# A fused top-k attention and feed-forward kernel: another order for the first pair's loads, transposes and scores

## The chip, the cores and the metric

The kernel runs on one core of one Trainium2 chip. The metric is the device time of one execution in microseconds (us); the number for the kernel before is the median of three runs. A profile comes with it: one execution recorded by the hardware profiler, in which times count from the start of the span. TensorE is called PE in it, VectorE DVE, ScalarE ACT, GpSimd POOL, and SyncE, which issues the transfers, SP.

## What is computed

Eight batches of eight heads, 576 positions and a head size of 64 go through an attention that keeps only the 32 largest scores of each row. The 4,608 rows that come out, 512 wide, go through a feed-forward with a gate.

```python
scores = scale * np.matmul(q, k.transpose(0, 1, 3, 2))
kth = np.partition(scores, -top_k, axis=-1)[..., -top_k:-top_k + 1]
scores = np.where(scores >= kth, scores, -1000000000.0)
attn = np.exp(scores - np.max(scores, axis=-1, keepdims=True))
attn = attn / (np.sum(attn, axis=-1, keepdims=True) + 1e-09)
x = np.matmul(attn, v)            # then (B, H, S, D) -> (B*S, H*D)
h = x @ w_in
out = (h * np.clip(h + 3.0, 0.0, 6.0) / 6.0) @ w_out
```

Queries, keys and values are float32. The two weights reach the kernel in eight bytes an element and are turned into float32 on the chip.

## The kernel before

**Pairs.** Two heads of a batch are a `Pair`. `load` (lines 146 to 158) brings its keys and queries into one tile, `landed`, with six transfers, all issued by SyncE: two heads of k, k's left rows, two heads of q, q's left rows. The 576 positions are 512 and 64 left over; the left rows of k and q share the ninth 128x128 tile of `landed`. `transpose` (lines 171 to 183) turns the nine tiles on TensorE into one PSUM tile, `big`, of five banks, of which there is one. ScalarE then copies the columns out: 1,024 of them for the keys and queries (line 179), 64 of the queries' left part (line 180), and the keys' left part into `kr` (line 183, twice).

**Duos.** Two pairs of a batch and 128 query rows are a `Duo`. `scores` (lines 201 to 244) multiplies queries by the left keys (line 232) and by the 512 keys of each head (line 238) into `big`, and ScalarE copies the result into `sc` (line 239 for the 512 columns of each head, line 242 for the left ones). A row of `sc` that belongs to one head and one query is 576 wide.

**Top k.** `top` is VectorE's work: MAX8 finds the eight largest of a row (line 256), MATCH_REPLACE8 takes them out (line 260), four rounds for 32 values. Then GpSimd computes `shift`, ScalarE does `exp` and the sum `den`, VectorE its `inverse` (line 293), GpSimd the `weights` (lines 303 and 312), SyncE a transposing transfer (`flip`), ScalarE or GpSimd `join` (line 324), and TensorE `values` (line 344).

**Weights.** `convert` (lines 96 to 125) turns one chunk of 512 columns into float32 in four steps, and there are 32 chunks: sixteen of `w_in`, then sixteen of `w_out`. Step one issues the load of the words into a tile `st`. Step two computes `a` and `y` on ScalarE (lines 108 and 111) and clamps `a` on GpSimd (line 109). Step three shifts and merges bits on VectorE (lines 117 and 118). Step four adds the two on GpSimd (line 123). `a` and `y` come from the pool `g`, which has eight buffers and also holds the gates `g` of the feed-forward (line 378). `convert_step` moves several chunks on by one step: it adds the chunk that VectorE had in the step before, does step three for the next one, step two for a later one, and issues one more load with `land`.

**Order.** The order of the work is the program's own: every engine takes its instructions as they are written. After a start that is written out (lines 521 to 533), the main loop goes over the duos, and for each over eight rounds of `top`, four for each of the duo's two pairs. One such round, `8 * m + i`, is called a slot here. Each slot has a round of `top`, one `convert_step`, and parts of earlier duos at fixed distances (`early`, `usual`, `behind`, `soon`). `piece` puts pieces of the feed-forward into the slots as they become due. Three times before the loop `convert_step` is called, so in slot `s` the chunk `s + 1` is on VectorE, `s + 3` on ScalarE, and `s` is added.

Of the kernel before, what the change touches and what calls it, by code (L numbers as in the profile page):

```python
# [10 lines left out]
F32 = mybir.dt.float32  # L11
# [18 lines left out]
def kernel(  # L30
# [9 lines left out]
    nc = tc.nc  # L40
    P = nc.NUM_PARTITIONS
    B, H, S, D = q.shape
    DM, FF = moe_w_in.shape
    J = S // P
    JP = J * P
    R = S - JP
# [6 lines left out]
    def pool(name, bufs, **kw):  # L53
        return ctx.enter_context(tc.tile_pool(name=name, bufs=bufs, **kw))
# [12 lines left out]
    ps_w = pool("ps_w", 3, space=PSUM)  # L67
    ctx.enter_context(tc.manual_schedule())

    def const(shape, name):  # L70
        return consts.tile(shape, F32, tag=name, name=name)

    ident = const([P, P], "ident")
# [4 lines left out]
    w_out = const([P, NFC, DM], "w_out")  # L78
# [9 lines left out]
    def big():  # L88

        return ps_big.tile([P, 5 * 512], F32, tag="big", name="big")  # L90
# [48 lines left out]
    class Pair:  # L139
# [3 lines left out]
            self.b, self.hp = b, hp  # L143
            self.vm, self.vr, self.kr = vms[hp], vrs[hp], krs[b % 2 * NHP + hp]

        def load(self):
            h0 = 2 * self.hp
            t = self.landed = kqpool.tile([P, 2 * J + 1, 2, D], F32, tag="kq", name="landed")
            for i, src in enumerate((k, q)):
                for hh in range(2):  # L150
                    nc.sync.dma_start(
                        t[:, i * J : (i + 1) * J, hh, :],
                        src[self.b, h0 + hh, 0:JP, :].rearrange("(p j) d -> p j d", j=J),
                    )
                nc.sync.dma_start(
                    t[i * R : (i + 1) * R, 2 * J, :, :],
                    src[self.b, h0 : h0 + 2, JP:S, :].rearrange("h s d -> s h d"),
                )
# [9 lines left out]
                    self.vr[hh * R : (hh + 1) * R, hh, :], v[self.b, h0 + hh, JP:S, :]  # L168
                )

        def transpose(self):
            kq = kqpool.tile([P, JP + S], F32, tag="kq", name="kq")
            self.kT, self.qT = kq[:, 0:JP], kq[:, JP : JP + S]
            ps = big()
            for j in range(2 * J + 1):
                rows = self.landed[:, j, :, :].rearrange("p h d -> p (h d)")
                nc.tensor.transpose(ps[:, j * P : (j + 1) * P], rows, ident[:])
            c0 = 2 * JP
            nc.scalar.copy(kq[:, 0:c0], ps[:, 0:c0])
            nc.scalar.copy(kq[:, c0 : c0 + R], ps[:, c0 + R : c0 + 2 * R])  # L180
            for hh in range(2):
                d = slice(hh * D, (hh + 1) * D)
                nc.scalar.copy(self.kr[d, hh, :], ps[d, c0 : c0 + R])

    class Duo:

# [14 lines left out]
        def scores(self, us=(0, 1)):  # L201

            if us[0] == 0:
                self.sc = scpool.tile([P, 2, 2 * (S + R)], F32, tag="sc", name="sc")
                self.den = mpool.tile([P, 2, 2], F32, tag="den", name="den")
            sc, nu = self.sc[:, us[0] : us[-1] + 1, :], len(us)
            ps = big()
            heads = [slice(0, D), slice(D, P)]
            qs = slice(self.qt * P, min(self.qt * P + P, S))
            banks = ps[:, 0 : 4 * 512].rearrange("p (n s) -> p n s", s=512)  # L210
            left = ps[:, 4 * 512 :]
            if self.rest:


                quarters = [
                    (i, hh, d, heads[u ^ hh])
                    for i, u in enumerate(us)
                    for hh, d in enumerate(heads)
                ]
                for i, hh, d, to in quarters:  # L220
                    pr = self.pairs[us[i]]
                    nc.tensor.matmul(banks[to, i, :], pr.qT[d, qs], pr.kT[d, :])
                for i, hh, d, to in quarters:
                    pr = self.pairs[us[i]]
                    nc.tensor.matmul(banks[to, 2 + i, 0:R], pr.qT[d, qs], pr.kr[d, hh, :])
                nc.gpsimd.memset(sc[:, :, S : S + R], 0.0)
                nc.scalar.copy(sc[:, :, 0:JP], banks[:, 0:nu, :])
                nc.scalar.copy(sc[:, :, JP:S], banks[:, 2 : 2 + nu, 0:R])
                return
            for i, u in enumerate(us):  # L230
                pr = self.pairs[u]
                nc.tensor.matmul(
                    left[:, i * P : (i + 1) * P], pr.qT[:, qs], pr.kr[:].rearrange("p h r -> p (h r)")
                )
            for i, u in enumerate(us):
                pr = self.pairs[u]
                for hh, d in enumerate(heads):
                    nc.tensor.matmul(banks[:, 2 * i + hh, :], pr.qT[d, qs], pr.kT[d, :])  # L238
            nc.scalar.copy(  # L239
                sc.rearrange("p u (h s) -> p (u h) s", h=2)[:, :, 0:JP], banks[:, 0 : 2 * nu, :]  # L240
            )
            nc.scalar.copy(  # L242
                sc[:, :, JP : JP + P], left[:, 0 : nu * P].rearrange("p (u r) -> p u r", r=P)
            )

        def row(self, u, t):
            return self.sc[:, u, t * S : (t + 1) * S]
# [162 lines left out]
    duos = []  # L410
# [17 lines left out]
    left = 0  # L428
# [63 lines left out]
    def land(count=1):  # L492

        for _ in range(min(count, len(chunks))):
            c = convert(*chunks.pop(0))
            next(c)
            landing.append(c)

    def convert_step():


        for c in adding:
            next(c, None)
        adding.clear()
        if len(converting) >= 2 or not landing:
            for c in converting[:1]:
                next(c)
            adding.extend(converting[:1])
            del converting[:1]
        if landing:  # L510
            c = landing.pop(0)
            next(c)
            converting.append(c)
        land()

    def pair_at(m, first):

        b, at = divmod(m, per_batch)
        return pairs[b + 1][at - first] if b + 1 < B and 0 <= at - first < NHP else None

    first = pairs[0]
    first[0].load()
    land(2)
    first[1].load()
    first[0].transpose()
    convert_step()
    duos[0].scores((0,))
    convert_step()
    first[2].load()
    convert_step()  # L530
    first[1].transpose()
    duos[0].scores((1,))
    land()

# [28 lines left out]
    def parts(slot, late=None):  # L563

        for m, part in sorted(queued.get(slot, []), key=lambda x: x[1][:-1] != "shift"):
            if late is not None and (part[:-1] in ("inverse", "weights")) != late:
                continue
            if part == "values":
                values(m)
            elif part == "place":  # L570
                place(m)
            else:
                getattr(duos[m], part[:-1])(int(part[-1]))

    due = 0.0
    for m in range(ND + 3):
        u = duos[m] if m < ND else None
        for i in range(8):
            if u:
                u.top(i // 4, i % 4)  # L580
            if m < 4:
                parts(8 * m + i, False)
            convert_step()
            if m == 0 and i == 0:
                first[3].load()
            if m == 0 and i in (1, 2):
                first[i + 1].transpose()
            if i == (4 if m == 0 else 1) and m + 1 < ND:
                duos[m + 1].scores()
            if m < 4:  # L590
                parts(8 * m + i, True)
            else:
                parts(8 * m + i)
            if m == 0 and i in (1, 4):
                for p in duos[i // 4].pairs:
                    p.load_values()
            if i == 0:
                p = pair_at(m, 4)
                if p:
                    p.load()  # L600
            if i == 3 and u and u.pairs[0].b and 1 <= m % per_batch <= 2:
                for p in duos[m - 1].pairs:
                    p.load_values()
            if i == 5:
                p = pair_at(m, 5)
                if p:
                    p.transpose()

            due += ((left > 0) + (left >= 24) / 8 + (left >= 48) / 8) / (2 if u and u.rest else 1)
            piece(int(due))  # L610
            due -= int(due)
# [36 lines left out]
```

## Time and profile before

| | |
|---|---|
| time, median of three runs | 1577.45 us (1576.88 to 1578.07) |
| span of the profiled execution | 1576.1 us |
| busy: TensorE matmul | 1442.0 us (91%) |
| busy: VectorE | 1466.6 us (93%) |
| busy: ScalarE | 1097.2 us (70%) |
| busy: GpSimd | 1142.7 us (73%) |
| mean of a MAX8 on a row of 576 | 747 ns |
| first MAX8 | 13.73 us |

A row of the timeline gives the start, the length, the engine, the line, what is written from what, the shape, the count, and in brackets how long the engine had been idle and what ended that. A line of the waits gives who waited for whom, the total in us, the number of times, and the longest. A wait for several things is put down to what came last. Busy shares are means over stages with different limits, so the start and the weight conversion are read from their own stretches.

### The profile page before, as it was taken

The page shows a single profiled execution, that of the slowest core. Times are in us where ns is not written, and L with a number is a line of the kernel's source. Part 1 is how long each engine was busy: PE and PEld are TensorE (multiplying, and loading weights), DVE is VectorE, ACT ScalarE, POOL GpSimd, SP SyncE. Part 2 cuts the span into 40 slices and gives each one's busy share as a digit, 9 for nine tenths or more (in the row PEclk, how much of TensorE's full clock was granted, in tenths as well). Part 3 has the DMA queues.
Part 4 walks back from the last instruction along what each step waited for, and adds up shares of the span by engine and source line. Part 5 has one row for each costly group of instructions (what it writes and reads, how often), then busy time and mean ns, then how long its engine had stood idle before and what let it go on. Part 6 is the DMA issues. An engine that isn't in the chain of part 4 may idle for free.

```text
span 1576.1 us, 28787 instructions
## 1 busy us (share of the span) xinstructions
PE 1442.0 (91%) x10272; PEld 1031.7 (65%) x10272; DVE 1466.6 (93%) x3105; ACT 1097.2 (70%) x1865; POOL 1142.7 (73%) x1264
## 2 busy tenths in 40 slices
PE   5355799879999999998999999998999999999899
PEld 3142666567767777676777777776777777776675
DVE  6999999999999999999999999999999999999700
ACT  6675776777877777777776786777776786777521
POOL 4868687777867777867687777867687777867831
PEclk9577899989999999999999999999999999999999
DMA  8552544444444543545254544445254443533410
GB/s 237 158 183 42 116 83 83 89 94 98 73 96 86 101 84 78 99 87 117 54 104 81 98 88 83 94 91 113 58 105 81 98 88 82 103 58 68 83 22 14
DMA packets 450319, 144.49 MB, mean 92 GB/s; under 512 B 433280, under 2 KB 441472, under 8 KB 450176
## 3 DMA queue, kind: packets, MB, share of 16 engines
q1 hardware_dynamic: 450176, 142.65, 43.7%
q8 instruction: 81, 1.33, 0.3%
q14 instruction: 62, 0.51, 0.1%
HBM read 45.09 MB, written 9.44 MB: 35 GB/s over the span
## 4 chain that ended last, share of the span: by engine, by line
DVE 74%; PE 12%; POOL 6%; issue 4%; ACT 2%; SPq 1%; DMA 1%; POOLq 0%
DVE m L256 39%; DVE wk L260 34%; PE acc L391 5%; PE h L371 5%; POOL e L312 1%; PE pv L344 1%; POOL a L109 1%; POOL sc L303 1%; ACT sc L284 1%; POOL w_in L123 1%; DVE den L293 1%; PE big L238 1%; POOL w_out L123 1%; DMA st<-in_moe_w_in_dram 1%; POOL eT L324 1%
## 5 line engine op out<-in xcount | busy, mean ns | idle before, releaser
L256 DVE MAX8 m<-wk 128x8 f32<-128x576 f32 x864 | 613.6, 747 | 2.2
L391 PE MATMUL acc<-w_out,g 128*128 128x512 f32 x1152 | 518.2, 601 | 18.1 <-POOL g L386 18.1
L371 PE MATMUL h<-xT,w_in 128*128 128x128 f32 x4096 | 482.9, 278 | 18.3 <-ACT xT L354 18.3
L371 PEld LDWEIGHTS h<-xT,w_in 128*128 128x128 f32 x4096 | 472.5, 194 | 40.6 <-issue 18.4
L260 DVE MATCH_REPLACE8 wk<-m,wk 128x576 f32<-128x576 f32 x576 | 424.0, 743 | 0.0
L303 POOL TENSOR_SCALAR sc<-sc,den 128x576 f32<-128x576 f32 x288 | 213.2, 750 | 241.2 <-DVE den L293 223.4
L391 PEld LDWEIGHTS acc<-w_out,g 128*128 128x128 f32 x1152 | 213.5, 191 | 265.5 <-issue 238.6
L312 POOL COPY e<-sc 128x2304 uint16<-128x2304 uint16 (+1 forms) x192 | 320.0, 1676 | 10.1
L279 ACT ACTIVATE sc<-sc,m 128x576 f32<-128x576 f32 x288 | 209.8, 774 | 76.3 <-DVE m L256 75.9
L284 ACT ACTIVATE sc<-sc,shift 128x576 f32<-128x576 f32 x288 | 220.2, 767 | 52.1 <-POOL shift L272 50.0
L324 ACT COPY eT<-t 128x2304 uint16<-128x2304 uint16 (+1 forms) x82 | 216.0, 2634 | 44.5 <-DMA t<-e 39.8
L344 PE MATMUL pv<-eT,vm 128*64 128x128 f32 (+1 forms) x2560 | 164.1, 273 | 58.7 <-ACT eT L324 44.0
L260 DVE MATCH_REPLACE8 wk<-m,sc 128x576 f32<-128x576 f32 x288 | 212.0, 743 | 0.0
L344 PEld LDWEIGHTS pv<-eT,vm 128*64 128x64 f32 x2560 | 135.1, 141 | 110.3 <-ACT eT L324 48.2
L324 POOL COPY eT<-t 128x2304 uint16<-128x2304 uint16 (+1 forms) x78 | 203.6, 2610 | 4.5 <-DMA t<-e 4.3
L256 DVE MAX8 m<-sc 128x8 f32<-128x576 f32 x288 | 203.4, 744 | 1.5 <-ACT sc L242 1.5
L386 POOL TENSOR_TENSOR g<-g,hs 128x512 f32<-128x512 f32 x144 | 184.8, 1283 | 12.1
L379 ACT ACTIVATE g<-h,three 128x512 f32<-128x512 f32 x144 | 98.3, 683 | 133.8 <-PE h L371 123.1
L238 PE MATMUL big<-kq 64*128 64x512 f32 x512 | 136.1, 651 | 0.0
L239 ACT COPY sc<-big 128x2048 f32<-128x2048 f32 (+1 forms) x65 | 119.2, 1833 | 17.4 <-PE big L238 17.2
L385 POOL TENSOR_SCALAR g<-g 128x512 f32<-128x512 f32 x144 | 89.0, 618 | 51.9 <-ACT g L379 40.7
L401 ACT ACTIVATE o<-acc 128x512 f32<-128x512 f32 x36 | 21.4, 594 | 89.1 <-PE acc L391 89.1
(47 smaller groups left out, 1087.3 us busy)
## 6 DMA issues: line engine op xcount, KB each, us to landing
landed<-in_k_dram SPq DMA_DIRECT2D x64, 128.0 KB, 2.9
landed<-in_q_dram SPq DMA_DIRECT2D x64, 128.0 KB, 2.9
st<-in_moe_w_in_dram SPq DMA_DIRECT2D x16, 512.0 KB, 5.0
vm<-in_v_dram SPq DMA_DIRECT2D x64, 128.0 KB, 2.3
st<-in_moe_w_out_dram SPq DMA_DIRECT2D x16, 512.0 KB, 6.2
out_dram<-o SPq DMA_DIRECT2D x32, 256.0 KB, 2.4
t<-e SPq DMA_TRANSPOSE x160, 4.6
landed<-in_k_dram SPq DMA_DIRECT2D x32, 32.0 KB, 2.5
```

The source lines that it names most:

```text
L238: nc.tensor.matmul(banks[:, 2 * i + hh, :], pr.qT[d, qs], pr.kT[d, :])
L256: nc.vector.max(self.m[u][:, t, 8 * r : 8 * r + 8], self.cur[t])
L260: nc.vector.match_replace(wk, self.m[u][:, t, 8 * r : 8 * r + 8], self.cur[t], LOWEST)
L279: nc.scalar.activation(row, row, AF.Prelu, bias=m[:, t, TOP_K - 1 : TOP_K], scale=-1.0, alpha=FLAT)
L284: nc.scalar.activation(row, row, AF.Exp, bias=self.less[u][:, t : t + 1], scale=-scale / FLAT, accum_out=self.den[:, u, t : t + 1],)
L303: nc.gpsimd.tensor_scalar(row, row, self.den[:, u, t : t + 1], 1.0, ALU.mult, ALU.mult)
L312: nc.gpsimd.tensor_copy(halves[:, :, to : to + c1 - c0], words)
L324: copy(eT[:, 0 : self.nb, :] .rearrange("p c q -> p (c q)") .bitcast(U16) .rearrange("p (x h) -> p h x", h=2), self.t16[u][:, 0 : 2 * self ...
L344: nc.tensor.matmul(pv[hh * D : (hh + 1) * D, u * w : (u + 1) * w], pr.vm[:, hh, c, :] if c < J else pr.vr[:, hh, :], rhs, start=(c == 0), ...
L371: nc.tensor.matmul(h[:, (f - f0) * P : (f - f0 + 1) * P], w_in[:, i, f * P : (f + 1) * P], xT[:, i, :], start=(i == 0), stop=(i == NHP - 1),)
L386: nc.gpsimd.tensor_tensor(g[:], g[:], hs[:], ALU.mult)
L391: nc.tensor.matmul(acc[:], gs[f // nf][:, f % nf * P : (f % nf + 1) * P], w_out[:, f, :], start=(f == 0), stop=(f == NFC - 1),)
```

## The change

It touches the start of the kernel, before the main loop is in its steady order. It is meant to let VectorE begin its top-k earlier, with TensorE out of its slow clock by the first scores and the first batch's keys and queries at hand. It does six things.

- The first pair's queries are issued by ScalarE's queue while SyncE issues its keys.
- A warm-up is put first: VectorE clears a part of `w_out`, and TensorE multiplies it with itself twice. The result is not used.
- The first pair is transposed into three tiles of the pool `ps_w` in place of `big`: keys, then the first queries together with the left tile, then the other queries. Only what the first scores need is copied at once; the other two copies (`later`) come after the scores.
- For the first half of the first duo the left scores are copied first and each head's 512 columns by themselves, so that VectorE can begin with one head.
- The loads of all four pairs of the first batch stand ahead of most weight chunks: pair 1 and pair 2 before the second chunk, pair 3 before the loop and not in slot 0.
- `convert_step` is called twice before the loop and not three times.

```diff
--- before.py
+++ after.py
@@ -143,16 +143,17 @@
             self.b, self.hp = b, hp
             self.vm, self.vr, self.kr = vms[hp], vrs[hp], krs[b % 2 * NHP + hp]
 
-        def load(self):
+        def load(self, queue=None):
+
             h0 = 2 * self.hp
             t = self.landed = kqpool.tile([P, 2 * J + 1, 2, D], F32, tag="kq", name="landed")
-            for i, src in enumerate((k, q)):
+            for i, (src, eng) in enumerate(((k, nc.sync), (q, queue or nc.sync))):
                 for hh in range(2):
-                    nc.sync.dma_start(
+                    eng.dma_start(
                         t[:, i * J : (i + 1) * J, hh, :],
                         src[self.b, h0 + hh, 0:JP, :].rearrange("(p j) d -> p j d", j=J),
                     )
-                nc.sync.dma_start(
+                eng.dma_start(
                     t[i * R : (i + 1) * R, 2 * J, :, :],
                     src[self.b, h0 : h0 + 2, JP:S, :].rearrange("h s d -> s h d"),
                 )
@@ -168,19 +169,41 @@
                     self.vr[hh * R : (hh + 1) * R, hh, :], v[self.b, h0 + hh, JP:S, :]
                 )
 
-        def transpose(self):
+        def transpose(self, first=False):
+
             kq = kqpool.tile([P, JP + S], F32, tag="kq", name="kq")
             self.kT, self.qT = kq[:, 0:JP], kq[:, JP : JP + S]
+            c0 = 2 * JP
+
+            def turn(ps, tiles):
+                for i, j in enumerate(tiles):
+                    rows = self.landed[:, j, :, :].rearrange("p h d -> p (h d)")
+                    nc.tensor.transpose(ps[:, i * P : (i + 1) * P], rows, ident[:])
+
+            def copy_left(ps):
+                for hh in range(2):
+                    d = slice(hh * D, (hh + 1) * D)
+                    nc.scalar.copy(self.kr[d, hh, :], ps[d, 0:R])
+
+            if first:
+
+                ps = [ps_w.tile([P, 512], F32, tag="w", name="kqp") for _ in range(3)]
+                turn(ps[0], range(J))
+                turn(ps[1], [J, 2 * J])
+                turn(ps[2], range(J + 1, 2 * J))
+                nc.scalar.copy(self.kT, ps[0][:])
+                nc.scalar.copy(kq[:, JP : JP + P], ps[1][:, 0:P])
+                copy_left(ps[1][:, P:])
+                self.later = [
+                    (kq[:, JP + P : c0], ps[2][:, 0 : JP - P]),
+                    (kq[:, c0 : c0 + R], ps[1][:, P + R : 2 * P]),
+                ]
+                return
             ps = big()
-            for j in range(2 * J + 1):
-                rows = self.landed[:, j, :, :].rearrange("p h d -> p (h d)")
-                nc.tensor.transpose(ps[:, j * P : (j + 1) * P], rows, ident[:])
-            c0 = 2 * JP
+            turn(ps, range(2 * J + 1))
             nc.scalar.copy(kq[:, 0:c0], ps[:, 0:c0])
             nc.scalar.copy(kq[:, c0 : c0 + R], ps[:, c0 + R : c0 + 2 * R])
-            for hh in range(2):
-                d = slice(hh * D, (hh + 1) * D)
-                nc.scalar.copy(self.kr[d, hh, :], ps[d, c0 : c0 + R])
+            copy_left(ps[:, c0:])
 
     class Duo:
 
@@ -236,12 +259,15 @@
                 pr = self.pairs[u]
                 for hh, d in enumerate(heads):
                     nc.tensor.matmul(banks[:, 2 * i + hh, :], pr.qT[d, qs], pr.kT[d, :])
-            nc.scalar.copy(
-                sc.rearrange("p u (h s) -> p (u h) s", h=2)[:, :, 0:JP], banks[:, 0 : 2 * nu, :]
-            )
-            nc.scalar.copy(
-                sc[:, :, JP : JP + P], left[:, 0 : nu * P].rearrange("p (u r) -> p u r", r=P)
-            )
+            copies = [
+                (sc.rearrange("p u (h s) -> p (u h) s", h=2)[:, :, 0:JP], banks[:, 0 : 2 * nu, :]),
+                (sc[:, :, JP : JP + P], left[:, 0 : nu * P].rearrange("p (u r) -> p u r", r=P)),
+            ]
+            if us == (0,):
+                (to, src), rest = copies
+                copies = [rest, (to[:, 0, :], src[:, 0, :]), (to[:, 1, :], src[:, 1, :])]
+            for copy in copies:
+                nc.scalar.copy(*copy)
 
         def row(self, u, t):
             return self.sc[:, u, t * S : (t + 1) * S]
@@ -519,16 +545,25 @@
         return pairs[b + 1][at - first] if b + 1 < B and 0 <= at - first < NHP else None
 
     first = pairs[0]
-    first[0].load()
-    land(2)
+
+
+    nc.vector.memset(w_out[:, 0, :], 0.0)
+    ps = big()
+    for _ in range(2):
+        nc.tensor.matmul(ps[:, 0:DM], w_out[:, 0, 0:P], w_out[:, 0, :])
+    first[0].load(nc.scalar)
     first[1].load()
-    first[0].transpose()
+    land()
+    first[2].load()
+    land()
+    first[0].transpose(first=True)
+    duos[0].scores((0,))
+    for copy in first[0].later:
+        nc.scalar.copy(*copy)
     convert_step()
-    duos[0].scores((0,))
+    first[3].load()
+    first[1].transpose()
     convert_step()
-    first[2].load()
-    convert_step()
-    first[1].transpose()
     duos[0].scores((1,))
     land()
 
@@ -581,8 +616,6 @@
             if m < 4:
                 parts(8 * m + i, False)
             convert_step()
-            if m == 0 and i == 0:
-                first[3].load()
             if m == 0 and i in (1, 2):
                 first[i + 1].transpose()
             if i == (4 if m == 0 else 1) and m + 1 < ND:
```

## The prediction

> **What bounds the kernel now.** I read the page's chain of waits first, then VectorE's waits, then the timeline of the first 14 us and of the stretch around 137 us.
>
> The chain by engine, from the page:
>
> ```profile
> DVE 74%; PE 12%; POOL 6%; issue 4%; ACT 2%; SPq 1%; DMA 1%; POOLq 0%
> ```
>
> VectorE (DVE) holds three quarters of the chain; the end is TensorE working off its queue after VectorE's last top-k. VectorE's waits over the whole span (total us, times, longest):
>
> ```profile
> DVE a L117 <- POOL a L109: 13.6, 2, 10.3
> DVE den L293 <- ACT den L289: 7.0, 2, 6.7
> DVE m L256 <- ACT sc L242: 1.5, 1, 1.5
> ```
>
> The 10.3 is before the first MAX8, 0.3 of the 7.0 is at 32.8 us, the 6.7 is in the tail, and 3.3 is at 137 us. Otherwise VectorE never idles, so a microsecond won before its first MAX8 is a microsecond of the total, unless a later wait takes it back. The start, in the timeline (start, length, what):
>
> ```profile
> 4.13 0.63 SPq L155 DMA_DIRECT2D landed<-in_q_dram  x1
> 4.45 1.09 PE L177 MATMUL big<-ident,landed 128*128 128x128 f32 x4 [4.45 <-DMA landed<-in_k_dram]
> 6.81 1.30 PE L177 MATMUL big<-ident,landed 128*128 128x128 f32 x5 [1.28 <-DMA landed<-in_q_dram]
> 8.15 1.01 ACT L179 COPY kq<-big 128x1024 f32<-128x1024 f32 x1 [6.15 <-PE big L177]
> 9.16 0.43 ACT L183 COPY kr<-big 64x64 f32<-64x64 f32 x2
> 9.69 0.77 PE L232 MATMUL big<-kr,kq 128*128 128x128 f32 x2 [1.58 <-ACT kr L183]
> 10.39 2.08 PE L238 MATMUL big<-kq 64*128 64x512 f32 x4
> 12.52 1.01 ACT L239 COPY sc<-big 128x1024 f32<-128x1024 f32 x1 [1.52 <-PE big L238]
> 13.43 0.27 ACT L242 COPY sc<-big 128x128 f32<-128x128 f32 x1
> 13.73 1.42 DVE L256 MAX8 m<-sc 128x8 f32<-128x576 f32 x2 [1.53 <-ACT sc L242]
> ```
>
> It is one serial chain: q's landing, transposes, copies, scores, copies, MAX8. Around 137 us, where the last weight chunks are converted:
>
> ```profile
> 134.52 0.69 ACT L379 ACTIVATE g<-h,three 128x512 f32<-128x512 f32 x1 [9.12 <-POOL w_out L123]
> 135.57 0.67 ACT L108 ACTIVATE a<-st 128x512 f32<-128x512 f32 x1
> 136.40 0.61 POOL L109 TENSOR_SCALAR a<-a 128x512 f32<-128x512 f32 x1 [1.91 <-ACT a L108]
> 137.05 1.49 DVE L117 TENSOR_SCALAR a<-a 128x512 uint32<-128x512 uint32 x1 [3.30 <-POOL a L109]
> 139.87 1.99 PE L238 MATMUL big<-kq 64*128 64x512 f32 x8
> 142.83 1.41 DVE L256 MAX8 m<-wk 128x8 f32<-128x576 f32 x2
> 144.01 2.52 POOL L123 TENSOR_TENSOR w_out<-a,y 128x512 int32<-128x512 int32 x2
> 144.16 1.40 DVE L256 MAX8 m<-sc 128x8 f32<-128x576 f32 x2
> ```
>
> Here the gates g and the conversion's a and y compete for the eight g buffers: three chunks in flight (six) and two g fill them, so ScalarE sits 9.12 us until an add (L123) frees one, the next chunk's clamp is late, and VectorE waits 3.30. This stretch matters below.
>
> **What the Trainium skill says.** "TensorE: Matmul & The Clock Gate", Part 1: TensorE starts at half clock and is released after a busy window of about 3.4 us that is free-running; that is what the warm-up is for. The trace agrees: four L238 take 2.08 us at 10.39, eight take 1.99 at 139.87. Part 4 there says that transposes hardly count as busy for that gate; no row here shows it. "DMA: Bandwidth & Descriptors", section "Issuing engines are not separate DMA queues": a second issuing engine saves only issue time, the same 16 engines carry the data. "SBUF — State Buffer", section "Who interferes with whom": some VectorE forms and GpSimd lock each other out for a whole instruction; here L117 takes 0.41 at its shortest and 1.49 beside a GpSimd add.
>
> **The change, part by part.**
>
> *q on ScalarE's queue.* Issues cost about 0.64 us each on SyncE; six end at 4.76 and TensorE has q at 6.81, 2.05 later. Two queues of three end at 2.77, so 4.8. By bandwidth: 157 GB/s at a share of 0.69 (window 3 to 4 us) is 228 GB/s at full share, 576 KB take 2.5 us from about 2.2, so 4.7. I take 5.0. If ScalarE issues only after its table load (1.28 us from 0.72) it is 6.1; the load's row carries the line of the first copy, so I expect it behind the issues.
>
> *Warm-up.* A 128x512 memset on VectorE is bounded by its rows of that shape, 0.41 and 0.68; done at 1.5. Two float32 matmuls of 512 columns are four passes; a pass of L238 is about 0.85 cold (two heads' passes run side by side, so its four take 2.08): to 4.95. Both are beside the loads. k's four transposes follow, 1.09, to 6.05; q's first and the left tile about 0.45 more, to 6.5. ScalarE copies k (512 columns; 1.01 for 1024 and 0.27 for 128 give 0.59) 6.05 to 6.65, then q's 128 columns and two kr, 0.48 (0.43 before with 64), to 7.15. The other four transposes' columns are copied later, off the path.
>
> *Scores and split copies.* L183's end to L238's start is 0.80 cold, about 0.4 warm; L238 2.08 cold, half of 1.99 plus 0.1 = 1.1 warm. The left copy now hides under L238, and MAX8 needs just one head's 512 columns: 0.05 + 0.59 + 0.03, against 1.01 + 0.27 in sequence. First MAX8: 7.15 + 0.4 + 1.1 + 0.67 = 9.3 warm, 10.7 cold. The window's phase and the transposes decide; I take 9.8. **Gain 13.73 - 9.8 = 3.9.**
>
> *Loads ahead, slots 0 to 4* (a slot is one pass of the inner loop). SyncE issues: k of pair 0 to 2.8, pair 1 to 6.7, chunk 0 to 7.3, pair 2 to 11.3, chunks 1 and 2 to 12.4, pair 3 to 16.4, chunk 3 to 17.0. It lands 2.05 + about 0.8 later, 19.8; at the 5.0 us median of the page from its issue, 21.4. Behind that wait on ScalarE stand pair 2's copies (1.45), nine transposes on TensorE (2.18), pair 3's copies (1.45) and exp (29.58 to 32.77, 3.2): 19.8 + 1.15 + 1.45 + 2.18 + 1.45 + 3.2 = 29.2. VectorE reaches its first reciprocal at 9.8 + (32.5 - 13.73) = 28.6, less about 0.6 for conversions that meet fewer GpSimd adds: 28.0. It waits 1.2, against 0.3. **Cost 0.9 - 0.6 = 0.3.**
>
> *One conversion step fewer ahead of the loop.* Two instead of three, so each chunk is converted one slot later. Before, chunk 0's L117 and L118 lay in VectorE's idle time (11.18); now all 32 pairs lie in the dense stretch, the last in slot 31, where there was none. 0.41 + 0.68 = 1.09 at least. Slots 23 to 30 keep their relations, so the 3.30 wait stays. But the last chunk's a now comes in slot 29, with six buffers held by two chunks and two g: it waits for slot 29's add, the first of the pair at 144.01, done 145.3. ScalarE to 146.0, GpSimd's clamp to 146.65. VectorE is there at 144.16: **wait 2.5, plus 1.09, plus contention with the next add (0 to 1.1; I take 0.5): 4.1.** Behind the waiting L117 stand all later MAX8. ScalarE's join at 141.94 slips too, but values come seven slots later.
>
> *Dropped load in slot 0, `later` copies:* beside VectorE's work, nothing.
>
> **Sum:** 1577.45 - 3.9 + 0.3 + 4.1 = 1578.0.
>
> **The rivals.**
> - *Start gain kept.* The last chunk finds its buffer in time and costs 1.1 to 1.7. For it: buffers may be handed out otherwise than I think. Against: the count above, and the same shortage at 134.52. 1577.45 - 3.9 + 0.3 + 1.4 = 1575.2; with a warm TensorE and no longer reciprocal wait 1574.0.
> - *The old wait goes too.* A chunk's shift loosens the knot at 137: another 3.3 less, 1571.9. Against: the same buffers are held in the same slots.
> - *Loads become the bound, slower.* Cold TensorE (gain 3.0), chunk 3 landing at 21.4 or later (reciprocal wait 1.5 more), full contention in slot 31 (4.7): 1577.45 - 3.0 + 1.8 + 4.7 = 1581.0. For it: from 10 to 30 us the DMA share is near 1.0 before already. Against: small packets are issued slower than 228 GB/s moves them.
>
> **How the numbers follow.** The forecast case has 0.58, the rivals 0.22, 0.07 and 0.13. Faster means under 1574.3, slower over 1580.6. The second rival, half of the first (if warm) and a little of the forecast case give 0.2; the third rival and the cold edge of the forecast 0.18; the rest 0.62. For 8 in 10 the range takes in the first rival and the lower edge of the third: 1574.0 to 1581.0.
>
> **What would show it.** Right: first MAX8 between 9.3 and 10.7 us; no SyncE issue of pair 3 after 17; a wait of L293 near 28 us of about 1; two waits of L117 on L109 between 130 and 145, of 3.3 and about 2.5, the second for the last chunk. Wrong: q reaching TensorE after 6 us, L238 still 2.08 us long, or only one such L117 wait (then the time is near 1575).

## The result and the profile after

The changed kernel takes 1581.72 us (median of six runs, 1580.52 to 1582.62), the kernel before on the same chip 1577.40 (six runs, 1576.88 to 1578.07). The ratio is 1.0027, with a 95% interval of 1.0014 to 1.0040: the change makes the kernel about 4.3 us slower. The forecast was 1578.0 with a range to 1581.0.

The span of the profiled execution is 1579.2 us. The chain of waits by engine, from the page:

```profile
DVE 62%; PE 26%; POOL 4%; issue 3%; ACT 2%; SPq 1%; DMA 1%; POOLq 0%; ACTq 0%
```

The split of shares is no help here: TensorE's part grew from 12% to 26%, but VectorE's busy time is the same (1467.7 and 1466.6 us). VectorE's waits tell more (who waits for whom, total us, times, longest):

```profile
DVE den L319 <- ACT den L315: 9.1, 2, 6.7
DVE m L282 <- ACT sc L270: 8.3, 1, 8.3
DVE a L117 <- POOL a L109: 7.3, 4, 3.3
```

L319 is the reciprocal (L293 before), L282 is MAX8 (L256 before). The wait ahead of the first MAX8 is shorter, as intended. New are three short waits of L117 beside the old 3.3, and 2.3 us of L319 where there was 0.3. The start, from the timeline (start, length, what, and in brackets the idle time and its end):

```profile
1.47 3.78 PE L553 MATMUL big<-w_out 128*128 128x512 f32 x4 [1.47 <-DVE w_out L550]
5.44 1.24 PE L181 MATMUL kqp<-ident,landed 128*128 128x128 f32 x9 [0.19 <-DMA landed<-in_k_dram]
6.17 0.59 ACT L194 COPY kq<-kqp 128x512 f32<-128x512 f32 x1 [2.12 <-PE kqp L181]
7.73 1.13 PE L261 MATMUL big<-kq 64*128 64x512 f32 x4
8.91 1.24 ACT L270 COPY sc<-big 128x128 f32<-128x128 f32 x3 [1.67 <-PE big L261]
```

The warm-up holds: nine transposes take 1.24 us, and four L261 1.13 where L238 took 2.08. The first MAX8 is at 9.69 us, against 13.73. VectorE from there to slot 5, from its own timeline:

```profile
13.70 0.43 DVE L117 TENSOR_SCALAR a<-a 128x512 uint32<-128x512 uint32 x1 [1.14 <-POOL a L109]
...
17.87 0.43 DVE L117 TENSOR_SCALAR a<-a 128x512 uint32<-128x512 uint32 x1 [0.37 <-POOL a L109]
...
31.93 0.17 DVE L319 RECIPROCAL den<-den 128x2 f32<-128x2 f32 x1 [2.34 <-ACT den L315]
32.01 1.40 DVE L282 MAX8 m<-wk 128x8 f32<-128x576 f32 x2
```

Slot 5 starts at 32.01 us, and before it started at 32.89. Of a start won by 4.04 us, 0.88 is left. What ScalarE does ahead of that reciprocal, from its timeline:

```profile
22.41 0.66 ACT L108 ACTIVATE a<-st 128x512 f32<-128x512 f32 x1 [2.33 <-DMA st<-in_moe_w_in_dram]
...
23.54 0.99 ACT L204 COPY kq<-big 128x1024 f32<-128x1024 f32 x1
...
24.98 0.69 ACT L108 ACTIVATE a<-st 128x512 f32<-128x512 f32 x1
...
27.23 1.01 ACT L204 COPY kq<-big 128x1024 f32<-128x1024 f32 x1 [0.99 <-PE big L181]
...
28.70 1.44 ACT L305 ACTIVATE sc<-sc,m 128x576 f32<-128x576 f32 x2
...
31.69 0.20 ACT L315 ACTIVATE den<-den 128x2 f32<-128x2 f32 x1
```

It is one chain in program order: chunk 3 lands (22.39 us), pair 2's copies, pair 3's transposes and copies, exp, `den`. Around 140 us, in the whole timeline:

```profile
136.14 1.49 DVE L117 TENSOR_SCALAR a<-a 128x512 uint32<-128x512 uint32 x1 [3.31 <-POOL a L109]
...
143.09 1.26 POOL L123 TENSOR_TENSOR w_out<-a,y 128x512 int32<-128x512 int32 x1
...
144.38 0.67 ACT L108 ACTIVATE a<-st 128x512 f32<-128x512 f32 x1 [3.24 <-POOL w_out L123]
...
145.13 0.61 POOL L109 TENSOR_SCALAR a<-a 128x512 f32<-128x512 f32 x1 [0.78 <-ACT a L108]
...
145.78 1.49 DVE L117 TENSOR_SCALAR a<-a 128x512 uint32<-128x512 uint32 x1 [2.44 <-POOL a L109]
...
147.19 0.68 DVE L118 SCALAR_TENSOR_TENSOR y<-st,y 128x512 uint32<-128x512 uint32 x1
147.79 1.41 DVE L282 MAX8 m<-sc 128x8 f32<-128x576 f32 x2
```

The old wait stays (in slot 29), and the last chunk has one of its own in slot 31: ScalarE may write `a` only when the add at 143.09 has given a buffer back. Slot 32 starts at 147.79, before at 144.16.

### The profile page after: what moved, and what is told of

The parts are those of the page before. It is cut to its first block, busy times and chain, and to the rows that moved or that the text cites. A ratio compares the mean times of both kernels' runs of the same rounds, so it can differ in the third digit from the quotient of the medians.

```text
span 1579.2 us, 28800 instructions
## 1 busy us (share of the span) xinstructions
PE 1447.5 (92%) x10276; PEld 1036.7 (66%) x10276; DVE 1467.7 (93%) x3106; ACT 1097.7 (70%) x1868; POOL 1141.9 (72%) x1264
## 4 chain that ended last, share of the span: by engine, by line
DVE 62%; PE 26%; POOL 4%; issue 3%; ACT 2%; SPq 1%; DMA 1%; POOLq 0%; ACTq 0%
DVE m L282 32%; DVE wk L286 27%; PE acc L417 10%; PE h L397 10%; PE pv L370 3%; PE big L261 2%; DVE y L118 1%; POOL e L338 1%; DVE a L117 1%; POOL g L412 1%; POOL sc L329 1%; POOL eT L350 1%; DMA t<-e 1%; SPq L152 1%; ACT sc L310 1%
## 5 line engine op out<-in xcount | busy, mean ns | idle before, releaser
L282 DVE MAX8 m<-wk 128x8 f32<-128x576 f32 x864 | 612.9, 746 | 2.2
L397 PE MATMUL h<-xT,w_in 128*128 128x128 f32 x4096 | 489.1, 281 | 18.5 <-ACT xT L380 18.5
L397 PEld LDWEIGHTS h<-xT,w_in 128*128 128x128 f32 x4096 | 478.7, 196 | 40.7 <-ACT xT L380 18.5
L338 POOL COPY e<-sc 128x2304 uint16<-128x2304 uint16 (+1 forms) x192 | 320.0, 1677 | 10.1
L282 DVE MAX8 m<-sc 128x8 f32<-128x576 f32 x288 | 203.2, 742 | 8.3 <-ACT sc L270 8.3
L270 ACT COPY sc<-big 128x256 f32<-128x256 f32 (+3 forms) x131 | 136.9, 1099 | 17.2 <-PE big L261 17.0
L261 PE MATMUL big<-kq 64*128 64x512 f32 x512 | 133.6, 641 | 0.0
L427 ACT ACTIVATE o<-acc 128x512 f32<-128x512 f32 x36 | 21.4, 594 | 92.5 <-PE acc L417 92.5
```

What stands on the lines that cost most here:

```text
L282: nc.vector.max(self.m[u][:, t, 8 * r : 8 * r + 8], self.cur[t])
L338: nc.gpsimd.tensor_copy(halves[:, :, to : to + c1 - c0], words)
L397: nc.tensor.matmul(h[:, (f - f0) * P : (f - f0 + 1) * P], w_in[:, i, f * P : (f + 1) * P], xT[:, i, :], start=(i == 0), stop=(i == NHP - 1),)
```

## The experiments

All readings below stand on one measure: when the first MAX8 of a slot starts on VectorE, as a difference to the kernel before. VectorE's work after slot 32 is the same in all, and so the last column goes through to VectorE's last MAX8 within 0.1 us. From there to the end of the span it takes 88.0 to 89.2 us, and 86.4 in d2. The slots of a kernel come from one profiled execution, whose time lies up to 1.8 us from the median. Times are medians; the difference is to the kernel before, run on the same chip in the same session (1577.40 for the first row, 1578.24, 1578.13 and 1578.29 for the three groups of four). Between kernels of different groups a time is therefore sure to about 1 us only; the slots are finer, except that landings at the start vary from one execution to the next: a2 and a3 are the same program up to slot 12, and their slot 5 differs by 0.89. A difference below that at slot 5 shows nothing.

| kernel | time | to before | ratio, 95% interval | slot 0 | slot 5 | slot 8 | slot 30 | slot 32 |
|---|---|---|---|---|---|---|---|---|
| before, start in us | | | | 13.73 | 32.89 | 45.02 | 139.13 | 144.16 |
| changed | 1581.72 | +4.3 | 1.0014 to 1.0040 | -4.04 | -0.88 | -0.87 | -0.90 | +3.63 |
| a1_step_back | 1579.23 | +1.0 | 1.0000 to 1.0017 | -3.57 | -0.68 | -0.68 | +1.17 | +1.17 |
| a2_loads_back | 1580.83 | +2.6 | 1.0009 to 1.0024 | -3.50 | -0.57 | -0.56 | -0.52 | +4.02 |
| a3_both_back | 1578.33 | +0.1 | 0.9993 to 1.0010 | -3.76 | -1.46 | -1.46 | +0.49 | +0.50 |
| a4_before_two_steps | 1582.07 | +3.8 | 1.0016 to 1.0037 | -0.07 | -0.10 | -0.09 | -0.09 | +4.46 |
| b1_exp_ahead_of_pair3 | 1580.68 | +2.6 | 1.0009 to 1.0023 | -3.24 | -3.45 | -2.30 | -2.22 | +2.34 |
| b2_no_warm_up | 1581.69 | +3.6 | 1.0014 to 1.0034 | -1.68 | -0.95 | -0.95 | -1.00 | +3.53 |
| b3_q_on_sync | 1583.86 | +5.7 | 1.0024 to 1.0049 | -3.56 | +1.36 | +1.36 | +1.32 | +5.85 |
| c1_ten_g_buffers | 1576.03 | -2.1 | 0.9982 to 0.9995 | -1.99 | -0.30 | -0.30 | -4.25 | -1.56 |
| d1_before_ten_g | 1576.13 | -2.2 | 0.9980 to 0.9993 | -0.28 | +0.39 | +0.39 | -3.56 | -1.60 |
| d2_ten_g_exp_ahead | 1574.58 | -3.7 | 0.9970 to 0.9987 | -3.36 | -2.82 | -1.70 | -5.62 | -2.91 |
| e1_three_steps_ten_g | 1571.53 | -6.8 | 0.9949 to 0.9974 | -3.04 | -3.75 | -3.73 | -7.61 | -5.66 |
| d4_before_y_in_place | 1578.88 | +0.6 | 0.9994 to 1.0011 | -0.11 | -0.02 | +0.03 | -1.66 | +0.27 |

The table splits the changed kernel's 3.63: -4.04 at the first MAX8, +3.16 between it and slot 5, nothing from slot 5 to slot 30, +4.53 in slots 30 and 31. The first theory was that these last two are separate costs, the one of the loads' order and the other of the missing step.

**The missing step, put back in a later slot.**

```diff
+            if m == 1 and i == 4:
+                convert_step()
```

> The changed kernel with one more conversion step in slot 12, so that from there on every chunk stands in the slot it had before the change and the last is on VectorE in slot 30. Theory (two separate costs, the missing step about 4.5 us and the loads ahead about 3.2 us): the wait of L117 on L109 near 145.8 us (2.44) goes, the 3.3 near 136 stays, the waits of the first 35 us stay; time 1581.7 - 3.5 to 4.5 = 1577.2 to 1578.2. The loads' order alone makes both waits: the second wait stays, 1581 to 1582. TensorE's lower clock is the cost: 1581 to 1582 whatever the waits do.

The wait of slot 31 is gone and the old one stays, as the theory says. The gain is smaller than expected, 2.46 at slot 32 and 2.5 to 3.3 in the time, since the extra step is not free either: slot 13 comes 2.60 later, of which 0.71 is made up by slot 15. Two of its rows in VectorE's timeline show it, a wait for the clamp and a L117 of 1.49 beside a GpSimd add, where the shortest takes 0.41:

```profile
65.27 1.49 DVE L117 TENSOR_SCALAR a<-a 128x512 uint32<-128x512 uint32 x1 [0.51 <-POOL a L109]
66.68 0.68 DVE L118 SCALAR_TENSOR_TENSOR y<-st,y 128x512 uint32<-128x512 uint32 x1
```

The mean granted clock is 0.955 here, 0.952 in the changed kernel and 0.962 before; the time follows the slots and not the clock.

**The loads in the order of before.**

```diff
     first[0].load(nc.scalar)
+    land(2)
     first[1].load()
-    land()
-    first[2].load()
-    land()
     first[0].transpose(first=True)
...
-    first[3].load()
+    first[2].load()
     first[1].transpose()
...
+            if m == 0 and i == 0:
+                first[3].load()
```

> The changed kernel with the loads in the order of before (two chunks ahead of pair 1, pair 2 after the first conversion step, pair 3 in slot 0); warm-up, three banks and queries on ScalarE's queue stay, and two conversion steps ahead of the loop. Theory of two costs: first MAX8 stays near 9.7; the waits of L117 at 13.7 and 17.9 us and the 2.3 of the first reciprocal go or fall under 0.7 together; the 2.44 in slot 31 stays; 1581.7 - 2.5 to 3.5 = 1578.2 to 1579.2. If the two queues or the warm-up make the chunks late and not the order: the early waits stay, 1581 to 1582. If the order makes the slot-31 wait as well: that goes too, 1574 to 1575.

A miss. The two early waits of L117 are gone, but the reciprocal now waits 2.87 us, and slot 5 starts 0.57 before that of the kernel before (1.46 in a3, whose start is the same), where it was 0.88 with the loads ahead. The time falls by 0.9 (between the medians) or 1.7 (as differences to the kernel before), not by 2.5 to 3.5. The timelines of ScalarE and VectorE say why:

```profile
23.64 0.66 ACT L111 ACTIVATE y<-st 128x512 f32<-128x512 uint32 x1
27.54 1.01 ACT L204 COPY kq<-big 128x1024 f32<-128x1024 f32 x1 [3.25 <-PE big L181]
...
29.01 1.44 ACT L305 ACTIVATE sc<-sc,m 128x576 f32<-128x576 f32 x2
...
32.23 0.17 DVE L319 RECIPROCAL den<-den 128x2 f32<-128x2 f32 x1 [2.87 <-ACT den L315]
```

Chunk 3 is early now, and pair 3 is late: its keys reach TensorE at 25.28, and exp stands behind its copies. Whichever of the two comes last, both are ahead of exp on ScalarE's queue. So the loads' order is at most a small part of the cost; the theory had to be mended: what counts is the last landing that exp stands behind.

**Both.** The edits of the two kernels above together.

> Both at once: loads in the order of before and one more conversion step in slot 12. Theory of two costs: they add, so 1581.7 - 3.0 - 4.0 = 1574.2 to 1575.7, faster than the kernel before by 2 to 3 us; that is the start's own gain. If one cause makes both waits, no better than the better of the two alone, 1577 to 1578. If TensorE's lower clock is the cost: 1581.

Between the medians the two gains add up (2.5 and 0.9 less than the changed kernel alone, 3.4 together; as differences to the kernel before 3.3, 1.7 and 4.2), but the result is the time of the kernel before and no better: most of the start that VectorE wins is still lost at the reciprocal (a wait of 2.32), and the extra step costs 1.89 in slots 12 to 14, as in a1. Its granted clock, 0.948, is below the changed kernel's 0.952, and its median is 3.4 us lower: the lower clock is not what costs the time.

**The missing step alone, on the kernel before.**

```diff
     duos[0].scores((0,))
-    convert_step()
     first[2].load()
     convert_step()
```

> The kernel before with two conversion steps ahead of the loop in place of three, and nothing else. Theory of two costs: first MAX8 as before or up to 0.5 us earlier, a second wait of L117 on L109 of about 2.4 for the last chunk in slot 31; 1577.4 + 4 to 5 = 1581.4 to 1582.4. If the loads' order makes that wait: 1577 to 1578. If the chunk has only its own 1.1 us of work there: 1578.5.

The expectation holds. With nothing else changed, slots 30 and 31 lose 4.55 us and the time rises by 3.8. VectorE's timeline of it:

```profile
142.74 1.41 DVE L256 MAX8 m<-wk 128x8 f32<-128x576 f32 x2
146.60 1.50 DVE L117 TENSOR_SCALAR a<-a 128x512 uint32<-128x512 uint32 x1 [2.45 <-POOL a L109]
148.02 0.68 DVE L118 SCALAR_TENSOR_TENSOR y<-st,y 128x512 uint32<-128x512 uint32 x1
```

**Pair 3 behind exp.** The mended theory says that exp is late because pair 3's transposes and copies stand ahead of it.

```diff
-            if m == 0 and i in (1, 2):
-                first[i + 1].transpose()
+            if m == 0 and i in (1, 3):
+                first[(i + 3) // 2].transpose()
```

> The changed kernel with pair 3 transposed in slot 3, behind the first exp on ScalarE's queue, in place of slot 2, ahead of it; loads as in the changed kernel. Theory: the first reciprocal (slot 4) ends a chain on ScalarE of chunk 3's landing, pair 2's copies, pair 3's transposes and copies, exp; without pair 3 in it exp begins near 26.2 in place of 28.7, the wait of 2.34 falls under 0.5, slot 5 starts near 29.8 in place of 32.0 and the time falls by 1.8 to 2.4, to about 1579.5; the two waits in slots 30 and 31 stay. If the wait comes from chunk 3's landing alone, or from exp's own length: slot 5 at 31.5 to 32, 1581 to 1582. If pair 3 then comes late for the second duo: a new wait in slot 8, 1581 or more.

The mechanism is right: exp starts at 25.99 in place of 28.70, the reciprocal no longer waits, and slot 5 starts 3.45 ahead of the kernel before, so 2.57 more of the start is kept.

```profile
25.99 1.43 ACT L305 ACTIVATE sc<-sc,m 128x576 f32<-128x576 f32 x2
...
29.36 0.15 DVE L319 RECIPROCAL den<-den 128x2 f32<-128x2 f32 x1
```

Of this 1.15 is given back in slots 6 and 7, so the gain at slot 32 is 1.29. That of the time is 1.0 between the medians and 1.7 as differences to the kernel before; 1.8 to 2.4 were expected. Slot 6 shows what is given back:

```profile
35.90 1.81 DVE L117 TENSOR_SCALAR a<-a 128x512 uint32<-128x512 uint32 x1
37.63 1.75 DVE L118 SCALAR_TENSOR_TENSOR y<-st,y 128x512 uint32<-128x512 uint32 x1
```

The same pair takes 1.01 and 1.75 in the changed kernel, and in slot 7 L117 takes 1.16 here and 0.74 there. GpSimd is copying and adding in those microseconds (L338 at 35.32, L123 at 37.39). The Trainium skill, "SBUF — State Buffer", "Who interferes with whom", has some VectorE forms and GpSimd lock each other out for a whole instruction; the rows agree, up to 1.81 against 0.41.

**No warm-up.**

```diff
-    nc.vector.memset(w_out[:, 0, :], 0.0)
-    ps = big()
-    for _ in range(2):
-        nc.tensor.matmul(ps[:, 0:DM], w_out[:, 0, 0:P], w_out[:, 0, :])
```

> The changed kernel without the memset and the two matmuls of the warm-up. Theory: L261 takes about 2.1 again and the first MAX8 comes near 11 in place of 9.7, but slot 5 stays near 32 since the chain on ScalarE sets it (the reciprocal's wait falls from 2.34 to 1 to 1.5), and the time stays within 0.5 of the changed kernel's, about 1581.7. If the early start is worth its time: 1583. If the warm-up itself costs (a lower granted clock afterwards): 1580 or less.

The first MAX8 is 2.36 us later than in the changed kernel, and slot 5 is not later at all; nor is the time. TensorE's timeline has the cold lengths:

```profile
6.11 2.15 PE L181 MATMUL kqp<-ident,landed 128*128 128x128 f32 x9 [6.11 <-DMA landed<-in_k_dram]
8.44 0.76 PE L255 MATMUL big<-kr,kq 128*128 128x128 f32 x2 [0.18 <-ACT kr L186]
```

So in the changed kernel the warm-up brings the first MAX8 forward and brings no time.

**All of the first pair on SyncE.**

```diff
-    first[0].load(nc.scalar)
+    first[0].load()
```

> The changed kernel with all six loads of the first pair issued by SyncE, as before. Theory: the queries land near 6.9 in place of 5.7, the first MAX8 comes 0.8 to 1.3 later, chunk 3 lands within 0.5 of 22.4 since the same bytes move, slot 5 stays near 32, time about 1581.7 within 0.5. If the two queues make the chunks late: chunk 3 under 21 and 1580 or less.

A miss, and the most useful one. The first MAX8 comes only 0.48 later than in the changed kernel, but chunk 3 is used at 24.65 in place of 22.41, slot 5 starts 2.24 later, and the total follows. The stretches 2 to 8 and 8 to 22 us of this kernel, and then of the changed one (busy time by engine, then granted clock, DMA share, GB/s):

```profile
2.00:8.00 6.00, 5.07 (x14) 2.23 (x13) 0.00 (x0) 1.16 (x4) 1.04 (x8) 1.00 0.65 146
8.00:22.00 14.00, 6.36 (x26) 3.40 (x26) 8.79 (x18) 7.75 (x17) 1.67 (x3) 0.68 0.97 228
```

```profile
2.00:8.00 6.00, 5.15 (x17) 2.28 (x17) 0.00 (x0) 2.34 (x5) 1.04 (x8) 1.00 0.84 188
8.00:22.00 14.00, 7.02 (x28) 3.78 (x26) 10.80 (x24) 7.83 (x17) 3.07 (x4) 0.66 1.02 251
```

With one queue the engines of the DMA are idle for a third of the stretch from 2 to 8 us, and they are not full before 12 us: the share is 0.66 from 8 to 10 us and 0.74 from 10 to 12 (0.88 and 1.11 in the changed kernel). SyncE issues without a gap in that time, about 0.6 us for each load, whether of 32 or of 128 KB, so the issues are the bound. By the GB/s of these stretches the DMA has moved about 0.5 MB less by 12 us, which at the 228 to 251 GB/s of the rows above is an estimated 2.0 to 2.2 us; after that the DMA is about full in both kernels and nothing is caught up. SyncE begins to issue chunk 3 at 19.87 in place of 17.82, and the loads just before it are late by as much. This shows the chain directly: chunk 3's landing moves by 2.2, slot 5 by 2.24, slot 32 by 2.22, the time by 1.4 (against before) or 2.1 (between the medians), while the first MAX8 moves by 0.5.

**Ten buffers in g.** The pools are full, so kq gives up one of its larger buffers.

```diff
-    kqpool = pool("kq", 14)
+    kqpool = pool("kq", 13)
...
-    gpool = pool("g", 8)
+    gpool = pool("g", 10)
```

> The changed kernel with ten buffers in the pool g in place of eight, and thirteen in kq in place of fourteen to make room. Theory (the waits of L117 in slots 30 and 31 come from a's and y's buffers that two gates hold): both waits, 3.3 and 2.44, go or fall under 0.5 together; the last chunk keeps its 1.1 to 2 us of work; 1581.7 - 5 to 6 = 1575.7 to 1576.7, if the thirteen buffers of kq cost nothing (a wait on kq would show as a later issue of a load). If late words or a late GpSimd make the waits: they stay, 1581.7.

Both waits are gone. From slot 8 to slot 32 this kernel gains 5.76 on the changed one (-1.26 against +4.50), as much as the two waits together (3.31 + 2.44), though not slot by slot: 3.92 up to slot 30 and 1.84 after it. The last chunk still has its own work in slot 31, 1.39 us, in VectorE's timeline:

```profile
141.21 0.41 DVE L117 TENSOR_SCALAR a<-a 128x512 uint32<-128x512 uint32 x1
141.53 1.15 DVE L118 SCALAR_TENSOR_TENSOR y<-st,y 128x512 uint32<-128x512 uint32 x1
142.60 1.41 DVE L282 MAX8 m<-sc 128x8 f32<-128x576 f32 x2
```

**Ten buffers in the kernel before.** The same edit there.

> The kernel before with ten buffers in g and thirteen in kq, nothing else. Theory (the 3.30 wait in slot 30 is a shortage of g buffers, with or without the change): that wait goes, 1577.5 - 2.8 to 3.5 = 1574 to 1574.7, so faster than the changed kernel with ten buffers (1576.0), since the change's own start is worth less than the last chunk's work in slot 31. If the shortage is the change's doing: 1577.5.

The 3.30 wait is gone there too, so the shortage is not the change's doing. From slot 8 to slot 32 it brings 2.0 and not 3.3: slot 30 starts 3.95 earlier and then takes 1.96 longer. Its L117 takes 1.30 and its L118 1.75 there, beside GpSimd's adds, where the kernel before has 0.41 and 0.68. With ten buffers both kernels take the same (1576.13 and 1576.03): the changed one is ahead by 0.69 at slot 8 and loses 0.73 from there to slot 32.

**Ten buffers and pair 3 behind exp**, on the changed kernel: the edits of b1 and c1 together.

> The changed kernel with both: ten buffers in g (thirteen in kq) and pair 3 transposed behind the first exp. Theory: the two parts are independent, so 1576.0 - 1.0 to 1.4 = 1574.6 to 1575.0; no wait of L117 between 130 and 150 us and none of the reciprocal near 30 us. If they share a cause: 1576.

They add: 1.35 better than ten buffers alone at slot 32, and 1574.58 us.

**A version that beats both.** What the runs priced is put together: the first pair's start of the change, the loads and the three steps of before (the first between the transposes and the first scores, so that chunk 0 has its VectorE work ahead of the first MAX8), pair 3 behind exp, ten buffers. Against the changed kernel, beside the edits shown above in the loop and the pools:

```diff
     first[0].load(nc.scalar)
+    land(2)
     first[1].load()
...
     first[0].transpose(first=True)
+    convert_step()
     duos[0].scores((0,))
     for copy in first[0].later:
         nc.scalar.copy(*copy)
     convert_step()
-    first[3].load()
+    first[2].load()
     first[1].transpose()
     convert_step()
```

> A version meant to beat both: warm-up, three banks, queries on ScalarE's queue and split copies of the change; loads in the order of before; three conversion steps ahead of the loop, the first between the transposes and the first scores; pair 3 transposed behind the first exp; ten buffers in g. Theory: first MAX8 at 11 to 12 (chunk 0 stands ahead of it again), last chunk back in slot 30, no wait of L117 near 137 or 145, no long wait of the first reciprocal; slot 5 at 30.5 to 31.5; 1577.5 - 3.3 - 1 to 2 = 1572.2 to 1573.2. If the start is worth nothing even so: 1574.2.

It takes 1571.53 us, 6.8 less than the kernel before and 10 to 11 less than the changed one. VectorE's waits are the whole story:

```profile
DVE a L117 <- POOL a L109: 8.3, 1, 8.3
DVE den L319 <- ACT den L315: 6.7, 1, 6.7
```

The first is the start (chunk 0 at 9.75 us, MAX8 at 10.69), the second is the tail, and between them VectorE never waits. Of the 3.04 us that its first MAX8 gains, all are still there at slot 8.

**One buffer of g for each chunk.** `y` is written over the low words it comes from.

```diff
-        y = gpool.tile([P, WC], F32, tag="g", name="y")
...
-        nc.scalar.activation(y[:], lo, AF.Copy, bias=2.0, scale=2.0**-51)
+        nc.scalar.activation(lo.bitcast(F32), lo, AF.Copy, bias=2.0, scale=2.0**-51)
...
-        au, yu = a[:].bitcast(U32), y[:].bitcast(U32)
+        au, yu = a[:].bitcast(U32), lo
...
```

> The kernel before with y written over the low words it is made from, in st, so that a chunk takes one buffer of g in place of two; g and kq keep eight and fourteen buffers. Theory of the shortage: the 3.30 wait goes as with ten buffers; L118 and the adds then read and write every second word, so they may take longer than 0.68 and 0.61 us each: 1574 if not, up to 1578 if L118 takes 0.1 us more in each of 32 slots.

The wait is gone with this too, which shows the shortage a second time and leaves kq alone. It brings nothing: what slot 30 gains is given back by slot 32. The merge of bits (line 117 here, 118 before) takes longer than in the kernel before, in the groups of VectorE to 150 us (busy us, mean ns), first this kernel and then before:

```profile
L117 DVE SCALAR_TENSOR_TENSOR st<-st 128x512 uint32<-128x512 uint32 x32 | 33.9, 1059 | 0.0
```

```profile
L118 DVE SCALAR_TENSOR_TENSOR y<-st,y 128x512 uint32<-128x512 uint32 x32 | 30.2, 944 | 0.0
```

The stride is not what makes the 115 ns. The shortest merge takes 0.68 us in both kernels, and over the first 25 chunks each merge takes the same in both within 0.03. Nearly all of the difference lies in the last seven chunks, where each slow merge has GpSimd beside it: that of the last chunk takes 2.58 in slot 30, beside a GpSimd copy of 2.17 at 140.46, where the kernel before has 0.68. These 1.9 us are what is given back by slot 32.

## Why the prediction was wrong

- **Start.** Right in mechanism. The first MAX8 was forecast at 9.8 and comes at 9.69; the gain of 3.9 is 4.04 at that point. The warm-up works and L261 is 1.13 (forecast 1.1). That the hit is so close is partly luck. The warm-up ends at 5.25 (forecast 4.95), TensorE gets its first tiles at 5.44, where the keys came at 4.45 before, and it makes up for that with nine warm transposes in 1.24, where 1.09 was forecast for the first four alone. And a1, b1, c1 and d2, whose start is the same but for the number of buffers in c1 and d2, have their first MAX8 at 10.16, 10.49, 11.74 and 10.37.
- **Loads ahead, slots 0 to 4.** This step failed, in size: a cost of 0.3 was forecast, 3.16 is measured. Of the 3.16, 1.51 are the two early waits of L117 and 2.05 the longer wait of the reciprocal (2.34, where 1.2 was forecast), less 0.4 for conversions that meet fewer adds (0.6 was forecast). The chain was named rightly, and its length from chunk 3's landing to the reciprocal is 9.5 us (22.39 to 31.93) where 9.4 was forecast. Wrong is the term where it begins: chunk 3 "lands 2.05 + about 0.8 later, 19.8". It lands at 22.39. SyncE begins to issue it at 17.82, where the forecast had 16.4: pair 2's and pair 3's last loads were held for 1.07 and 1.35 us in place of 0.63. And it takes 4.57 us from its issue, not 0.6 + 2.85. The rows of SyncE:

```profile
16.43 1.35 SPq L156 DMA_DIRECT2D landed<-in_q_dram  x1
...
17.82 2.02 SPq L102 DMA_DIRECT2D st<-in_moe_w_in_dram  x4
```

The forecast took the 2.05 of the first queries, which were under way while the DMA share was 0.58 (4 to 6 us), although its own next clause quoted the page's median of 5.0. It also set against a late chunk that small packets are issued slower than they are moved; that holds at the very start (b3), but with a DMA share of 1.02 from 8 to 22 us it does not hold for chunk 3.

b3 showed that the landings on this chain set the time, b2 that the first MAX8 does not. The order of the loads, to which the forecast put the cost, is at most a small part of it: with the order of before, a2 and a3 lose 2.93 and 2.30 over the same slots, since pair 3 then lands late (its keys reach TensorE at 25.28 and 24.46), and exp stands behind that too.

- **The waits of chunks 0 and 1** (1.14 and 0.37 in slots 0 and 1) were not forecast at all. They cost little by themselves, since VectorE would only have waited longer at the reciprocal: a2 and a3 are without them, and their slot 5 starts 0.57 and 1.46 ahead of before, in place of 0.88.
- **One conversion step fewer.** Right in mechanism and nearly in size: 4.1 forecast, 4.53 measured. The wait is 2.44 (forecast 2.5), the old one stays at 3.31, and the last chunk's own work costs 2.01 with the adds beside it in place of 1.09 + 0.5. a4 shows it alone on the kernel before, c1 shows that it is a shortage of buffers.
- **Sum.** -4.04 + 3.16 + 4.53 is 3.65, and slot 32 is 3.63 late. The forecast had +0.5. Of the 3.1 between them, 2.9 come from slots 0 to 4 and 0.4 from slot 31, less 0.1 at the start. Chunk 3's landing, 2.6 later than forecast, accounts for most of the 2.9.
- **Rivals.** Three of the four conditions of the slow rival came about or nearly so: chunk 3 landing after 21.4, a reciprocal wait longer by 1.5 (2.05 measured), near full contention in slot 31 (4.5 of 4.7). Only the cold TensorE did not, and b2 shows that it would not have mattered; so the rival did not need it. Its chance of 0.13 was far too small: the evidence for it, a DMA share near 1.0 before the change, was read and then argued away.

## What to carry to other kernels

A start that is won at the first instruction is worth only what the next wait leaves of it. Follow each engine's queue in program order to the first result that the busy engine needs back (here exp and its sum), and see which landing stands ahead of it; moving a piece that nobody needs yet behind that result may be worth more than a faster start (2.57 us more at slot 5 in b1, where the warm-up's 2.36 at the first MAX8 left nothing). Where the DMA share is near 1, price a landing by loads of its own size in that stretch (from issue to landing 4.4 to 5.2 us for the first four chunks of 512 KB here, and up to 7.4 for those issued right behind another), not by the first load of the kernel. Before a producer is shifted by one slot, count who holds the buffers in the last slots as well as in the first: eight buffers for three chunks and two gates were too few, and one more chunk in the dense stretch cost 4.5 us.

## What the runs showed of the hardware

- The second issuing queue was worth more than the earlier queries. The Trainium skill, "DMA: Bandwidth & Descriptors", "Issuing engines are not separate DMA queues", says that it saves only the time of issue; b3 agrees, but the time of issue was the bound while the DMA was filling: a share of 0.65 with one queue and 0.84 with two from 2 to 8 us, and 2.2 us at the end of the chain.
- The warm-up did not hold in every trace. In c1 TensorE was idle for 0.62 us between it and the first transposes, and these and the scores were cold, as the rows of TensorE show; in a1 it was idle for 0.72 and nine transposes took 1.17. What decides was not settled.

```profile
5.88 2.15 PE L181 MATMUL kqp<-ident,landed 128*128 128x128 f32 x9 [0.62 <-DMA landed<-in_k_dram]
8.17 0.76 PE L255 MATMUL big<-kr,kq 128*128 128x128 f32 x2
8.86 2.04 PE L261 MATMUL big<-kq 64*128 64x512 f32 x4
```

- The granted clock does not tell whether TensorE is warm in this stretch. The nine transposes of pair 2 take 2.18 us in both kernels, at 22.18 us before and at 19.00 after, and it reads 1.00 from 22 to 24 us before and 0.50 from 18 to 20 after. Warm ones took 1.20 (pair 1 in the changed kernel).
- A wait that is taken away can come back as contention. With ten buffers the kernel before loses its 3.30 wait, and its slot 30 takes 1.96 us more, all of it in L117 and L118 beside GpSimd's adds. In d4 one merge of bits takes 1.9 us more in the same slot.
